# A decode kernel with two attention layers and two small mixers: earlier layer-norm statistics, mixers in halves, 50 idle matmuls and rearranged small constants

## The chip, the cores and the metric

The kernel runs on one core of a Trainium2 chip. Time is device time in microseconds (us). In the views, PE is TensorE, which runs the matmuls, PEld its weight loads (a matmul and its weight load are called a pair below), DVE VectorE, ACT ScalarE, SP the engine that issues the loads, and DMA the 16 engines that carry them out. A "span" is the length of the one profiled execution of a kernel; it is some 1.8 us shorter than the time reported for that execution (539.3 against 541.08 us before). A ratio is the mean time of a kernel's fast runs over that of the kernel before in the same rounds on the same chip, so it is not quite the ratio of the medians quoted beside it. A profile or a chain shows one execution, which need not be the typical one.

## The reference

One token (`x` of 640 values) passes through attention, mixer, attention, mixer, each with a layer norm. Attention uses the last 4096 positions of a cache of 32 heads with 192 values each, so each layer reads 32 K slabs and 32 V slabs of 1.5 MB. Both layers have the same cache and weights.

```python
def _A_ref(x, k_cache, v_cache, wq, wo):           # cut
    q = (x @ wq) ...                               # 32 heads of 192
    k = k_cache[:, :, Sk - W:, :]                  # W = 4096
    v = v_cache[:, :, Sk - W:, :]
    p = softmax(einsum("bhqd,bhkd->bhqk", q, k) * Dh ** -0.5)
    return einsum("bhqk,bhkd->bhqd", p, v) ... @ wo
def _B_ref(x, w1, w2, w3, w4):                     # with S = 1 the shifted parts are zero: x1 = x
    h2 = _gelu(_layernorm(x1) @ w3) @ w4
    return x1 + h2
x = x + _A_ref(_layernorm(x), ...); x = x + _B_ref(_layernorm(x), ...)   # twice
```

## The kernel before

Everything that comes from memory lands in eleven "cells" of 12,288 bytes per partition, handed out again when their reader is done; the query weights and part of the mixer weights have places of their own. Seven transposed K slabs are kept from layer 0 for layer 1. In SBUF the small constants lie ahead of the cells.

```python
const = ctx.enter_context(tc.tile_pool(name="const", bufs=1))
cells = ctx.enter_context(tc.tile_pool(name="cells", bufs=1))      # after const, in SBUF too
wq_sb = const.tile([P, ND, HD], BF16, name="wq_sb")
...
even = const.tile([P, 1], F32, name="even")      # 4 bytes take 32 here: see a_minus32
lo = const.tile([P, 1], F32, name="lo")
maskq = const.tile([P, 4], F32, name="maskq")
blkm = const.tile([P, NM], F32, name="blkm")
...
def give(key):                                   # a cell is free again: the next load may start
    free.append(cell_of.pop(key))
...
def mixer(layer, x_cur, rs_cur, x_new, rs_new):
    xc, xcf, total = ln_center(x_cur, rs_cur)    # mean by a fp32 matmul with ones, then x - mean
    for fc in range(NF):                         # NF = 12, ND = 5: 60 matmuls with w3
        for kc in range(ND):
            nc.tensor.matmul(hT_ps[:, fc:fc + 1], lhsT=w3[kc][...], rhs=xc[:, kc:kc + 1], ...)
        if fc == NF // 3:
            var_ps = total()                     # fp32 matmul: the variance
            rr = power(var_ps, 1.0 + eps, eps2, "rr")
    ...                                          # GELU by exp and reciprocals, on ScalarE and VectorE
    for n in range(ND):                          # 60 matmuls with w4
        for fc in range(NF):
            nc.tensor.matmul(y2_ps[:, n:n + 1], lhsT=w4[fc][...], rhs=hT[:, fc:fc + 1], ...)
```

## Time and profile before

| reading | before |
|---|---|
| time, median of the first 4 runs | 541.01 us (540.15 to 541.38) |
| span of the profiled execution | 539.3 us |
| transfer rate away from start, hand-over and end | 422 GB/s |
| hand-over from layer 0 to layer 1, slices 20 to 24 of 40 | 401, 404, 396, 331, 382 GB/s |
| start of the last output projection, when its last weights had landed, to the end | 10.4 us |

First the page of the kernel before: its span, the rows for busy DMA engines and moved GB/s (40 equal slices of the span), the data queue and the instruction queue (packets, MB, share of 16 engines' span), and the chain of waits by engine.

```profile
span 539.3 us, 14866 instructions
DMA  8999999999999999999999999999999999999992
GB/s 347 427 425 422 419 424 423 423 424 418 422 424 424 418 424 422 421 423 424 401 404 396 331 382 424 419 424 420 427 420 421 422 420 423 420 422 425 422 408 93
q1 hardware_dynamic: 23636, 218.54, 97.7%
q8 instruction: 53, 0.87, 0.7%
DMA 71%; PE 15%; DVE 11%; issue 2%; ACT 1%; SPq 0%; DVEq 0%; ACTq 0%
```

The DMA engines are full nearly everywhere (the data queue's packets fill 97.7% of their span).

In the hand-over the chain of waits of the kernel before (start, length, what) reads as follows. L482 is layer 0's last output projection, L703 mixer 0's second matmuls; "issue" is time in which PE waited for nothing that the profile shows.

```profile
288.43 0.98 PE y_ps L482 x30
...
294.34 1.75 PE y_ps L703 x60
296.29 0.28 issue
...
301.30 1.71 issue
...
306.94 1.45 issue
```

The timeline of the SP engine has the load of the next output-projection weights, which cannot start before layer 1's fourth head gives its cell back:

```profile
308.66 0.33 SPq L143 DMA_DIRECT2D cell<-in_A_wo_dram  x1
```

And the end of the chain: the last output-projection weights land at 528.82 us, then the last output projection (L482), the variance matmul (L288), the first GELU step (L680), the w4 matmuls (L703) and the final fp32 transpose (L721).

```profile
512.83 15.99 DMA cell<-in_A_wo_dram
528.87 0.58 PE y_ps L482 x15
...
531.34 0.43 PE var_ps L288 x2
...
532.79 0.28 ACT sq L680
...
534.35 1.75 PE y_ps L703 x60
...
536.43 0.39 PE row_ps L721
```

### The profile page before, as it was taken

To read this page: it belongs to the slowest core of one execution; us is meant where nothing else is said; L and a number is where in the kernel's file an instruction comes from. 1 tells how busy PE (TensorE), PEld (TensorE's weight loads), DVE (VectorE), ACT (ScalarE), POOL (GpSimd) and SP (SyncE) were. 2 spreads that over 40 slices of the span, in tenths; PEclk is the share of its full clock that TensorE was granted. 3 is DMA by queue.
4 is the path that set the end of the run, shared out by engine and by line. 5 is a ranking of instruction groups with operands and counts; after the bars stand their busy time and mean duration, and the time that the engine had idled before them with its cause. 6 is when DMAs were issued, how large, how long until landed. Compare 5 with 4: busy or idle time off the path is not lost.

```text
span 539.3 us, 14866 instructions
## 1 busy us (share of the span) xinstructions
PE 281.6 (52%) x6820; PEld 229.1 (42%) x6820; DVE 257.4 (48%) x494; ACT 54.6 (10%) x249; POOL 2.0 (0%) x11
## 2 busy tenths in 40 slices
PE   0146556364363644645635777665454654636555
PEld 0045445254353533534424765554343543525434
DVE  2187536455455545546303147665363654545511
ACT  1001010010100101010201011010010101001011
POOL 1000000000000000000000000000000000000000
DMA  8999999999999999999999999999999999999992
GB/s 347 427 425 422 419 424 423 423 424 418 422 424 424 418 424 422 421 423 424 401 404 396 331 382 424 419 424 420 427 420 421 422 420 423 420 422 425 422 408 93
DMA packets 23698, 219.48 MB, mean 407 GB/s; under 512 B 2517, under 2 KB 2901, under 8 KB 8149
## 3 DMA queue, kind: packets, MB, share of 16 engines
q1 hardware_dynamic: 23636, 218.54, 97.7%
q8 instruction: 53, 0.87, 0.7%
q14 instruction: 9, 0.07, 0.0%
HBM read 218.53 MB, written 0.00 MB: 405 GB/s over the span
## 4 chain that ended last, share of the span: by engine, by line
DMA 71%; PE 15%; DVE 11%; issue 2%; ACT 1%; SPq 0%; DVEq 0%; ACTq 0%
DMA cell<-in_A_k_cache_dram 49%; DMA cell<-in_A_v_cache_dram 15%; DVE cell L322 10%; PE O_ps L459 4%; PE ST_ps L372 3%; DMA cell<-in_A_wo_dram 3%; DMA wq_sb<-in_A_wq_dram 3%; PE qT_ps L339 1%; PE y_ps L482 1%; PE nb_ps L402 1%; PE hT_ps L671 1%; PE y_ps L703 1%; PE l_ps L422 1%; DVE o_sb L463 0%; PE PT_ps L417 0%
## 5 line engine op out<-in xcount | busy, mean ns | idle before, releaser
L322 DVE STREAM_TRANSPOSE cell<-cell 128x768 uint32<-128x768 uint32 x228 | 204.6, 946 | 91.5 <-DMA cell<-in_A_k_cache_dram 91.5
L372 PE MATMUL ST_ps<-Qblk,cell 128*128 128x4 bf16 x3072 | 113.4, 168 | 159.3 <-DVE cell L322 155.2
L372 PEld LDWEIGHTS <-cell 128*128 128x128 bf16 x3072 | 97.3, 105 | 189.8 <-DVE cell L322 181.0
L459 PE MATMUL O_ps<-cell,PT 128*1 128x192 bf16 x2048 | 98.3, 359 | 16.7 <-DMA cell<-in_A_v_cache_dram 16.2
L463 DVE STREAM_TRANSPOSE o_sb<-O_ps 128x192 f32<-128x192 f32 x64 | 24.5, 382 | 114.2 <-PE O_ps L459 114.2
L459 PEld LDWEIGHTS <-PT 128*1 128x1 bf16 x2048 | 68.6, 115 | 23.5 <-issue 12.3
L472 ACT ACTIVATE oT<-oT_ps,rl 32x6 bf16<-32x6 f32 x64 | 16.5, 257 | 284.8 <-PE oT_ps L471 284.8
L408 ACT ACTIVATE Pr<-ST_ps,nb_sb,sc 128x32 bf16<-128x32 f32 x64 | 25.1, 488 | 0.5
L471 PE MATMUL oT_ps<-o_sb,Lq 128*32 128x6 f32 x128 | 17.0, 204 | 11.8 <-DVE o_sb L463 11.7
L339 PE MATMUL qT_ps<-xc,wq_sb 128*128 128x1 bf16 x480 | 15.9, 166 | 13.4 <-DMA wq_sb<-in_A_wq_dram 12.9
L339 PEld LDWEIGHTS <-wq_sb 128*128 128x128 bf16 x480 | 15.0, 105 | 14.1 <-DMA wq_sb<-in_A_wq_dram 13.6
L471 PEld LDWEIGHTS oT_ps<-o_sb,Lq 128*32 128x32 f32 x128 | 12.0, 142 | 20.9 <-issue 15.6
L417 PEld LDWEIGHTS <-Eq 128*32 128x32 bf16 x256 | 4.0, 105 | 30.8 <-DVE y_acc L522 25.2
L482 PE MATMUL y_ps<-oT,cell 128*128 128x1 bf16 x480 | 15.3, 166 | 2.9 <-DMA cell<-in_A_wo_dram 1.9
L353 PE MATMUL Qrep_ps<-Xq,Lb 128*128 128x24 bf16 (+1 forms) x18 | 3.2, 180 | 25.3 <-DVE Xq L346 25.0
L482 PEld LDWEIGHTS <-cell 128*128 128x128 bf16 x480 | 14.6, 105 | 3.5 <-DMA cell<-in_A_wo_dram 2.6
L408 ACT ACTIVATION_READ_ACCUMULATOR Pr<-ST_ps,nb_sb,sc 128x1 f32 x64 | 14.4, 224 | 0.0
L404 ACT COPY nb_sb<-nb_ps 128x4 f32<-128x4 f32 x16 | 2.6, 162 | 112.0 <-PE nb_ps L402 112.0
L422 PE MATMUL l_ps<-lpart,ones 128*128 128x4 f32 x32 | 9.4, 365 | 5.3 <-ACT PT L420 5.3
L346 DVE TENSOR_TENSOR Xq<-qT_ps,maskq 128x24 bf16<-128x24 f32 (+1 forms) x18 | 2.8, 155 | 19.5 <-PE qT_ps L339 19.4
L422 PEld LDWEIGHTS l_ps<-lpart,ones 128*128 128x128 f32 x32 | 8.0, 311 | 6.9 <-ACT PT L420 6.7
L402 PE MATMUL nb_ps<-dg,ones 4*128 4x4 f32 x32 | 9.0, 348 | 1.0
(85 smaller groups left out, 107.0 us busy)
## 6 DMA issues: line engine op xcount, KB each, us to landing
cell<-in_A_v_cache_dram SPq DMA_DIRECT2D x59, 1536.0 KB, 28.0
cell<-in_A_k_cache_dram SPq DMA_DIRECT2D x57, 1536.0 KB, 28.1
cell<-in_A_wo_dram SPq DMA_DIRECT2D x14, 960.0 KB, 24.4
wq_sb<-in_A_wq_dram SPq DMA_DIRECT2D x5, 1536.0 KB, 11.0
cell<-in_A_v_cache_dram SPq DMA_DIRECT2D x9, 768.0 KB, 14.4
cell<-in_B_w_dram SPq DMA_DIRECT2D x2, 1280.0 KB, 14.5
cell<-in_A_wo_dram SPq DMA_DIRECT2D x4, 480.0 KB, 15.2
cell<-in_B_w_dram SPq DMA_DIRECT2D x1, 1536.0 KB
```

The costliest lines, as they stand in the source:

```text
L322: nc.vector.transpose(Tu, Ku[:, :, q * NY:(q + 1) * NY])
L339: nc.tensor.matmul(qT_ps[:, tl:tl + 1], lhsT=wq_sb[:, kc, t * P:(t + 1) * P], rhs=xc[:, kc:kc + 1], start=(kc == 0), stop=(kc == ND - 1))
L372: nc.tensor.matmul(ST_ps[:, hq, q * ng + g, :], lhsT=T4[:, g, f, :, t], rhs=Qblk[:, h * NCOL + 2 * f + t, :], start=(n == 0), stop=(n == N ...
L402: nc.tensor.matmul(nb_ps[:], lhsT=ones[0:n, :], rhs=held["dg"][0:n, :], start=True, stop=True)
L408: nc.scalar.activation(out=Pr[:, hq].rearrange("p m g -> p g m"), in_=ST_ps[:, hq], func=ACTF.Exp, bias=nb_sb[:, hq:hq + 1], scale=sc[:, 0 ...
L422: nc.tensor.matmul(l_ps[:], lhsT=ones[:], rhs=held["l"][:], start=True, stop=True)
L459: nc.tensor.matmul(O_ps[r:r + 1, :], lhsT=PT[:, hq, i:i + 1], rhs=V[:, i * Dh:(i + 1) * Dh], start=(i < 4), stop=(i >= NB - 4))
L463: nc.vector.transpose(o_sb[:], O_ps[:].rearrange("p (a c) -> p c a", c=NA))
L471: nc.tensor.matmul(oT_ps[r, :], lhsT=Lq[:], rhs=o_sb[:, :, 0], start=True, stop=True)
L472: nc.scalar.activation(oT[r, :], oT_ps[r, :], ACTF.Copy, scale=rl[r, 0:1])
L482: nc.tensor.matmul(y_ps[:, n:n + 1], lhsT=wo_t[:, k * D + n * P:k * D + (n + 1) * P], rhs=oT[:, k:k + 1], start=(i == 0 if split else k == 0),
L671: nc.tensor.matmul(hT_ps[:, fc:fc + 1], lhsT=w3[kc][:, f0:f0 + 2 * P - 1:2], rhs=xc[:, kc:kc + 1], start=(kc == 0), stop=(kc == ND - 1))
```

## The change

The intent is to shorten both mixers. The last output-projection sum is centred beforehand, so row sum and sum of squares come from a small remainder `z` and both fp32 matmuls stand ahead of the w3 matmuls. The w3 matmuls go in two halves to two PSUM tiles, so that the first half's GELU can overlap PE. The final transpose is bf16 instead of fp32. Fifty idle matmuls, whose results nothing reads, stand at the start. Some small constants share a tile, which makes room for new ones.

```diff
+NORM = (True, True)
+HALF = (True, True)
+BF16_OUT = True
+PAD = 50
 ...
-    even = const.tile([P, 1], F32, name="even")
-    lo = const.tile([P, 1], F32, name="lo")
-    maskq = const.tile([P, 4], F32, name="maskq")
-    blkm = const.tile([P, NM], F32, name="blkm")
+    el = const.tile([P, 2], F32, name="el")
+    even, lo = el[:, 0:1], el[:, 1:2]
+    mb = const.tile([P, 4 + NM], F32, name="mb")
+    maskq, blkm = mb[:, 0:4], mb[:, 4:4 + NM]
 ...
+    def idle_matmuls(n):
+        if n:
+            pad_ps = psm.tile([P, 1], F32, tag="psm")
+            for _ in range(n):
+                nc.tensor.matmul(pad_ps[:], lhsT=Lb[:], rhs=Lb[:, 0:1], start=True, stop=True)
+    idle_matmuls(PAD)
 ...                                       # in add_y: n is the number of sums still to come
+            if n == 1:                    # y so far, with its row sum; later centred to y[1]
+                nc.vector.scalar_tensor_tensor(out=y_new[:], in0=y_ps[:], ..., accum_out=rs[:, 0:1])
+            if n == 0:
+                nc.vector.scalar_tensor_tensor(out=z_new[:], in0=y_ps[:], ..., in1=y[1][:], accum_out=rs_new[:, 0:1])
+                nc.scalar.activation(junk[:], z_new[:], ACTF.Square, accum_out=ss_new[:, 0:1])
 ...                                       # in mixer
+        nc.tensor.matmul(s1_ps[:], lhsT=ones[:], rhs=rs_cur[:, 0:1], start=True, stop=True)
+        nc.tensor.matmul(s2_ps[:], lhsT=ones[:], rhs=ss_cur[:, 0:1], start=True, stop=True)
 ...
+        for half in range(parts):         # two PSUM tiles, then GELU half by half
+            for i in range(HF): ...       # w3
+        order = [(n, half * HF + i) for half in range(parts) for n in range(ND) for i in range(HF)]
 ...
-    x1, x2, x3, x4 = (const.tile([P, ND], F32, name=f"x{i}") for i in range(1, 5))
-    rs1, rs2, rs3 = (const.tile([P, 1], F32, name=f"rs{i}") for i in range(1, 4))
+    x1, x2, x3 = (const.tile([P, ND], F32, name=f"x{i}") for i in range(1, 4))
+    x4 = const.tile([P, ND], out.dtype if BF16_OUT else F32, name="x4")
+    z = [const.tile([P, ND], F32, name=f"z{i}") ...]
+    zs = [const.tile([P, 1], F32, name=f"zs{i}") for i in range(4)]
```

More of the change, by code (lines that the diff above doesn't have):

```diff
@@ L30 @@
 NJ4, NGK, NM = 4, 8, 4
+NORM = (True, True)
+HALF = (True, True)
+BF16_OUT = True
+PAD = 50
+PAD1 = 0
+HOLD = False
 @with_exitstack
@@ L257 @@
     nc.vector.memset(eps1[:], eps)
-    eps2 = const.tile([P, 1], F32, name="eps2")
-    nc.vector.memset(eps2[:], eps * eps)
+    if not all(NORM):
+        eps2 = const.tile([P, 1], F32, name="eps2")
+        nc.vector.memset(eps2[:], eps * eps)
+    for i in range(PAD1):
+        nc.vector.memset(const.tile([P, 1], F32, name=f"gap{i}")[:], 0.0)
     Qblk = const.tile([P, H * NCOL, NM], BF16, name="Qblk")
@@ L269, with shared @@
                             op1=ALU.add, accum_out=rs0[:, 0:1])
+    def shared(name, tag):
+        return dict(name=name, tag=tag) if any(NORM) and not all(HALF) else dict(name=name)
+    def idle_matmuls(n):
[4 more added lines that the diff above has]
+    idle_matmuls(PAD)
     def ln_center(x, rowsum):
@@ L291, in ln_center, with power @@
         return xc, xcf, total
-    def power(var_ps, mul, bias, tag):
+    def power(var, mul, bias, tag):
         ln_t = sm.tile([P, 1], F32, tag=tag + "_ln")
-        nc.scalar.activation(ln_t[:], var_ps[:, 0:1], ACTF.Ln, bias=bias[:], scale=mul / D)
+        nc.scalar.activation(ln_t[:], var, ACTF.Ln, bias=bias, scale=mul)
         r = sm.tile([P, 1], F32, tag=tag)
@@ L487, in out_proj, with attention @@
         return y_ps
-    def attention(layer, x_cur, rs_cur, x_new, rs_new):
+    def attention(layer, x_cur, rs_cur, x_new, z_new, rs_new, ss_new):
         groups = GROUPS[layer]
@@ L492, in attention @@
         y = [x_cur]
+        junk = sm.tile([P, ND], F32, tag="ln_junk")
         Th = {}
@@ L498, in softmax_scale @@
         def softmax_scale():
-            rstd = power(total(), 1.0, eps1, "rstd")
+            rstd = power(total()[:, 0:1], 1.0 / D, eps1[:], "rstd")
             nc.vector.tensor_scalar(out=sc[:], in0=rstd[:], scalar1=scale, scalar2=None, op0=ALU.mult)
@@ L514, in S, with add_y, center @@
                 area[0] = None
-        def add_y(y_ps, last):
-            if last:
-                nc.vector.scalar_tensor_tensor(out=x_new[:], in0=y_ps[:], scalar=1.0, in1=y[0][:],
-                                               op0=ALU.mult, op1=ALU.add, accum_out=rs_new[:, 0:1])
-                return
-            y_new = sm.tile([P, ND], F32, name="y_acc")
-            nc.vector.tensor_add(y_new[:], y[0][:], y_ps[:])
+        def add_y(y_ps, n):
+            if not NORM[layer]:
+                if n == 0:
+                    nc.vector.scalar_tensor_tensor(out=x_new[:], in0=y_ps[:], scalar=1.0, in1=y[0][:],
+                                                   op0=ALU.mult, op1=ALU.add, accum_out=rs_new[:, 0:1])
+                    return
+                y_new = sm.tile([P, ND], F32, name="y_acc")
+                nc.vector.tensor_add(y_new[:], y[0][:], y_ps[:])
+                y[0] = y_new
+                return
+            y_new = x_new if n == 0 else sm.tile([P, ND], F32, name="y_acc")
+            if n == 1:
+                rs = sm.tile([P, 1], F32, **shared("rs_y", "ln_ssq"))
+                nc.vector.scalar_tensor_tensor(out=y_new[:], in0=y_ps[:], scalar=1.0, in1=y[0][:],
+                                               op0=ALU.mult, op1=ALU.add, accum_out=rs[:, 0:1])
+                def center():
+                    nm_ps = psm.tile([P, 1], F32, tag="psm")
+                    nc.tensor.matmul(nm_ps[:], lhsT=ones[:], rhs=rs[:, 0:1], start=True, stop=True)
+                    ym = sm.tile([P, ND], F32, **shared("y_m", "xcf"))
+                    nc.vector.scalar_tensor_tensor(out=ym[:], in0=nm_ps[:, 0:1].broadcast_to([P, ND]),
+                                                   scalar=-1.0 / D, in1=y_new[:], op0=ALU.mult, op1=ALU.add)
+                    y.append(ym)
+                y.append(center)
+            else:
+                if n == 0:
+                    nc.vector.scalar_tensor_tensor(out=z_new[:], in0=y_ps[:], scalar=1.0, in1=y[1][:],
+                                                   op0=ALU.mult, op1=ALU.add, accum_out=rs_new[:, 0:1])
+                    nc.scalar.activation(junk[:], z_new[:], ACTF.Square, accum_out=ss_new[:, 0:1])
+                nc.vector.tensor_add(y_new[:], y[0][:], y_ps[:])
@@ L523, in add_y, with center_y @@
             y[0] = y_new
+        def center_y():
+            if NORM[layer]:
+                y.pop()()
         qa, qb = (qproj_steps(groups[0][0] // QH, xc, part) for part in (0, 1))
@@ L602, in attention @@
                     if pending is not None:
-                        add_y(y_ps, False)
+                        add_y(y_ps, 2)
                         pending = None
@@ L612, in attention @@
                 if layer == 0:
-                    add_y(out_proj(layer, *pending), False)
+                    add_y(out_proj(layer, *pending), 1)
                 PT, rl = early
@@ L621, in attention @@
                 if final:
+                    if layer == 0 and hq == 1:
+                        center_y()
                     fold = None
@@ L655, in attention @@
                 if layer == 1:
-                    add_y(out_proj(layer, *pending), False)
-                fold()
+                    y_ps = out_proj(layer, *pending)
+                    if not NORM[1]:
+                        add_y(y_ps, 1)
+                    fold()
+                    if NORM[1]:
+                        add_y(y_ps, 1)
+                    center_y()
+                else:
+                    fold()
             pending = (cur[0] // QH, oT)
             ST = ST_n
-        add_y(out_proj(layer, *pending), True)
@@ L662, in mixer @@
-    def mixer(layer, x_cur, rs_cur, x_new, rs_new):
+        add_y(out_proj(layer, *pending), 0)
+    def mixer(layer, x_cur, z, rs_cur, ss_cur, x_new, rs_new):
         w3 = need("w3", 0)
-        xc, xcf, total = ln_center(x_cur, rs_cur)
-        hT_ps = psm.tile([P, NF], F32, tag="psm")
-        for fc in range(NF):
-            f0 = 2 * P * (fc // 2) + fc % 2
-            for kc in range(ND):
-                nc.tensor.matmul(
-                    hT_ps[:, fc:fc + 1], lhsT=w3[kc][:, f0:f0 + 2 * P - 1:2], rhs=xc[:, kc:kc + 1],
-                    start=(kc == 0), stop=(kc == ND - 1))
-            if fc == NF // 3:
-                var_ps = total()
-                rr = power(var_ps, 1.0 + eps, eps2, "rr")
-        rg = sm.tile([P, 1], F32, name="rg")
-        nc.vector.tensor_scalar(out=rg[:], in0=rr[:], scalar1=GELU_A * GELU_C, scalar2=None, op0=ALU.mult)
-        sq = sm.tile([P, NF], F32, name="sq")
-        nc.scalar.activation(sq[:], hT_ps[:], ACTF.Square, scale=rr[:, 0:1])
-        gu = sm.tile([P, NF], F32, name="gu")
-        nc.vector.scalar_tensor_tensor(out=gu[:], in0=sq[:], scalar=1.0 / GELU_C, in1=hT_ps[:],
-                                       op0=ALU.add, op1=ALU.mult)
-        ge = sm.tile([P, NF], F32, name="ge")
-        nc.scalar.activation(ge[:], gu[:], ACTF.Exp, scale=rg[:, 0:1])
-        rh = sm.tile([P, NF], F32, name="rh")
-        nc.vector.tensor_scalar(out=rh[:], in0=hT_ps[:], scalar1=rr[:, 0:1], scalar2=None, op0=ALU.mult)
-        nc.vector.reciprocal(rh[:], rh[:])
-        hT = sm.tile([P, NF], BF16, name="hT")
-        nc.vector.scalar_tensor_tensor(out=gu[:], in0=ge[:], scalar=1.0, in1=rh[:],
-                                       op0=ALU.add, op1=ALU.mult)
-        rstd = power(var_ps, 1.0, eps1, "rstd")
-        with nc.allow_low_precision(reason="the matmul's operand, bf16 as in the reference"):
-            nc.vector.reciprocal(hT[:], gu[:])
@@ new lines, in mixer @@
+        stats = []
+        if NORM[layer]:
+            s1_ps = psm.tile([P, 1], F32, tag="psm")
+            nc.tensor.matmul(s1_ps[:], lhsT=ones[:], rhs=rs_cur[:, 0:1], start=True, stop=True)
+            s2_ps = psm.tile([P, 1], F32, tag="psm")
+            nc.tensor.matmul(s2_ps[:], lhsT=ones[:], rhs=ss_cur[:, 0:1], start=True, stop=True)
+            xc = sm.tile([P, ND], BF16, name="xc")
+            xcf = sm.tile([P, ND], F32, name="xcf")
+            for t in (xc, xcf):
+                nc.vector.scalar_tensor_tensor(out=t[:], in0=s1_ps[:, 0:1].broadcast_to([P, ND]), scalar=-1.0 / D,
+                                               in1=z[:], op0=ALU.mult, op1=ALU.add)
+            st = sm.tile([P, 4], F32, **shared("st", "nb_sb"))
+            m2, s2d, b1, b2 = (st[:, i:i + 1] for i in range(4))
+            nc.vector.tensor_scalar(out=b1, in0=s1_ps[:], scalar1=1.0 / D, scalar2=None, op0=ALU.mult)
+            nc.vector.tensor_tensor(out=m2, in0=b1, in1=b1, op=ALU.mult)
+            nc.vector.tensor_scalar(out=b2, in0=m2, scalar1=-(1.0 + eps), scalar2=eps * eps, op0=ALU.mult, op1=ALU.add)
+            nc.vector.scalar_tensor_tensor(out=s2d, in0=s2_ps[:], scalar=1.0 / D, in1=m2, op0=ALU.mult, op1=ALU.max)
+            rr = power(s2d, 1.0 + eps, b2, "rr")
+            rg = sm.tile([P, 1], F32, **shared("rg", "sc"))
+            nc.vector.tensor_scalar(out=rg[:], in0=rr[:], scalar1=GELU_A * GELU_C, scalar2=None, op0=ALU.mult)
+            nc.vector.tensor_scalar(out=b1, in0=m2, scalar1=-1.0, scalar2=eps, op0=ALU.mult, op1=ALU.add)
+        else:
+            xc, xcf, total = ln_center(x_cur, rs_cur)
@@ new lines, in mixer @@
+        parts = 2 if HALF[layer] else 1
+        HF = NF // parts
+        hT = sm.tile([P, NF], BF16, name="hT")
+        h_ps = []
+        for half in range(parts):
+            if HALF[layer]:
+                hp = psS.tile([P, 4, NGK, NM], F32, name="ST_ps")
+                hp = hp[:, 0].rearrange("p g m -> p (g m)")[:, 0:HF]
+            else:
+                hp = psm.tile([P, NF], F32, tag="psm")
+            for i in range(HF):
+                fc = half * HF + i
+                f0 = 2 * P * (fc // 2) + fc % 2
+                for kc in range(ND):
+                    nc.tensor.matmul(
+                        hp[:, i:i + 1], lhsT=w3[kc][:, f0:f0 + 2 * P - 1:2], rhs=xc[:, kc:kc + 1],
+                        start=(kc == 0), stop=(kc == ND - 1))
+                if fc == NF // 3 and not NORM[layer]:
+                    var_ps = total()
+                    rr = power(var_ps[:, 0:1], (1.0 + eps) / D, eps2[:], "rr")
+            h_ps.append(hp)
@@ new lines, in mixer @@
+        if not NORM[layer]:
+            rg = sm.tile([P, 1], F32, **shared("rg", "sc"))
+            nc.vector.tensor_scalar(out=rg[:], in0=rr[:], scalar1=GELU_A * GELU_C, scalar2=None, op0=ALU.mult)
+        for half, hp in enumerate(h_ps):
+            WF = NF // 2 if all(HALF) else NF
+            sq, gu, ge, rh = (sm.tile([P, WF], F32, name=n)[:, 0:HF] for n in ("sq", "gu", "ge", "rh"))
+            nc.scalar.activation(sq, hp[:] if not HALF[layer] else hp, ACTF.Square, scale=rr[:, 0:1])
+            hpa = hp[:] if not HALF[layer] else hp
+            nc.vector.scalar_tensor_tensor(out=gu, in0=sq, scalar=1.0 / GELU_C, in1=hpa,
+                                           op0=ALU.add, op1=ALU.mult)
+            nc.scalar.activation(ge, gu, ACTF.Exp, scale=rg[:, 0:1])
+            nc.vector.tensor_scalar(out=rh, in0=hpa, scalar1=rr[:, 0:1], scalar2=None, op0=ALU.mult)
+            nc.vector.reciprocal(rh, rh)
+            nc.vector.scalar_tensor_tensor(out=gu, in0=ge, scalar=1.0, in1=rh,
+                                           op0=ALU.add, op1=ALU.mult)
+            with nc.allow_low_precision(reason="the matmul's operand, bf16 as in the reference"):
+                nc.vector.reciprocal(hT[:, half * HF:(half + 1) * HF], gu)
@@ L696, in mixer @@
+        if NORM[layer]:
+            rstd = power(s2d, 1.0, b1, "rstd")
+        else:
+            rstd = power(var_ps[:, 0:1], 1.0 / D, eps1[:], "rstd")
         base = sm.tile([P, ND], F32, name="base")
@@ L700, in mixer @@
         y2_ps = psm.tile([P, ND], F32, tag="psm")
-        for n in range(ND):
-            for fc in range(NF):
-                nc.tensor.matmul(
-                    y2_ps[:, n:n + 1], lhsT=w4[fc][:, n * P:(n + 1) * P], rhs=hT[:, fc:fc + 1],
-                    start=(fc == 0), stop=(fc == NF - 1))
+        order = [(n, half * HF + i) for half in range(parts) for n in range(ND) for i in range(HF)]
+        for i, (n, fc) in enumerate(order):
+            nc.tensor.matmul(
+                y2_ps[:, n:n + 1], lhsT=w4[fc][:, n * P:(n + 1) * P], rhs=hT[:, fc:fc + 1],
+                start=(i == 0 if HALF[layer] else fc == 0),
+                stop=(i == len(order) - 1 if HALF[layer] else fc == NF - 1))
         give(("w4", layer))
@@ L711, in mixer @@
                                            op0=ALU.mult, op1=ALU.add, accum_out=rs_new[:, 0:1])
-    x1, x2, x3, x4 = (const.tile([P, ND], F32, name=f"x{i}") for i in range(1, 5))
-    rs1, rs2, rs3 = (const.tile([P, 1], F32, name=f"rs{i}") for i in range(1, 4))
-    attention(0, xT, rs0, x1, rs1)
-    mixer(0, x1, rs1, x2, rs2)
-    attention(1, x2, rs2, x3, rs3)
-    mixer(1, x3, rs3, x4, None)
-    row_ps = psm.tile([ND, P], F32, tag="psm")
-    nc.tensor.transpose(row_ps[:, :], x4[:, :], ident[:, :])
+    x1, x2, x3 = (const.tile([P, ND], F32, name=f"x{i}") for i in range(1, 4))
+    x4 = const.tile([P, ND], out.dtype if BF16_OUT else F32, name="x4")
+    rs2 = const.tile([P, 1], F32, name="rs2")
+    z = [const.tile([P, ND], F32, name=f"z{i}") if NORM[i] else None for i in range(2)]
+    zs = [const.tile([P, 1], F32, name=f"zs{i}") for i in range(4)]
+    attention(0, xT, rs0, x1, z[0], zs[0], zs[1])
+    mixer(0, x1, z[0], zs[0], zs[1], x2, rs2)
+    attention(1, x2, rs2, x3, z[1], zs[2], zs[3])
+    mixer(1, x3, z[1], zs[2], zs[3], x4, None)
+    row_ps = psm.tile([ND, P], out.dtype if BF16_OUT else F32, tag="psm")
+    nc.tensor.transpose(row_ps[:, :], x4[:, :], Eq[:].rearrange("p j b -> p (j b)") if BF16_OUT else ident[:, :])
     o_fin = const.tile([ND, P], out.dtype, name="o_fin")
```

## The prediction

> **What bounds it now.** The span is 539.3 us. The queue part of the page has the data queue's packets at 97.7% of the 16 DMA engines' span; slices hold 420 to 425 GB/s except in two places. Slices 20 to 23 (the hand-over from layer 0 to layer 1) fall to 401, 404, 396, 331, 382; two-microsecond windows show 271 to 380 GB/s from 296 to 316 us, about 4.4 us of lost transfer. And the end: after the last output-projection weights land at 528.8 us, only compute is left, 10.5 us in the chain of waits. The change alters no bytes, so its gain can only come from those two places.
>
> **The tail, layer 1 (timeline).** Before: z/x at 529.47, mean matmul, xc, 60 w3 matmuls from 530.53 to 532.69 with the fp32 variance matmul costing 0.43 us in their midst, GELU chain 532.79 to 534.34 with PE idle 1.65 us, 60 w4 matmuls 1.75 us, x4 at 536.13, fp32 transpose 0.37 us, copy, DMA out. After: row sum and sum of squares come from a pre-centred z, so both fp32 matmuls go before the w3 matmuls, while PE waits for xc anyway (0.43 us gained; PE starts w3 at about the same time). Centring y takes one fp32 matmul (about 0.58 us) while the last projection weights are awaited, hence nothing. rr is known near 531.6, so the first half's GELU starts at about 531.65, 1.1 us earlier. The second half's chain follows on ACT and DVE and ends near 534.2; the first 30 w4 matmuls are hidden under it, leaving 30 (0.87 us) instead of 60. x4 near 535.1: 1.0 us gained. The bf16 transpose gives another 0.15 to 0.2. The w4 transfer ends at 532, so it doesn't hold the earlier start. Tail: about 1.15 us.
>
> **The hand-over.** Mixer 0 is on the chain too (288.4 to 296.3), and K/V transfers of layer 1 starve behind it, so its 1.0 us should reach the DMA. But here the chain has "issue" stalls of PE: 0.28 us before the mean matmul, 1.71 us at 301.3, 1.45 us at 306.9. Exactly 128 load/matmul pairs lie between them, so I read them as instruction fetch[...]. The 50 idle pairs at the start cost nothing (PE waits there for wq until 10.98 and 22.05 us), but move those boundaries 52 pairs earlier against the work: into w4, then the 17th and 65th pair-stretches of layer 1's first scores. My estimate is stalls of the same kind, total 2.5 to 4 us against 3.4. So the hand-over gains 0 to 2 us, probably 0.9.
>
> **Prediction.** 541.0 - 1.15 - 0.9, about 538.9 us; range 537.7 to 540.3. Faster by over 2%: 0.01; within 2%: 0.98; slower by over 2%: 0.01.
>
> **What would show it.** Chain of waits: from the last projection weights' landing to the end 9.3 to 9.4 us instead of 10.5; in the timeline first w4 matmul near 4.4 us after that landing (was 5.5), a second idle of PE before the second 30; transpose about 0.2 us. Windows of 2 us from the hand-over: less lost transfer; the last DMA landing about 0.9 us earlier. PE idle for "issue" at new positions, still 128 pairs apart. DMA bytes equal.
>
> **What would make it wrong.** Refill stalls falling into mixer 0 or adding up to more; a stall in the tail; the second half's GELU running serially behind the first longer than estimated; starvation in the hand-over that is set by the transposes rather than the mixer.

541.0 - 1.15 (tail) - 0.9 (hand-over) comes to 538.95 us. The trace of the kernel before shows a queue of the kind "instruction" (q8) with 53 packets of 16,384 bytes, one for each 257 of the 13,640 weight loads and matmuls that the page counts, and, by the matmul records, 128 pairs between the ends of the waits at 303.01 and 308.38 us. The 0.15 to 0.2 us for the transpose is an estimate: there the fp32 transpose took 0.37 us (L721), a bf16 transposing matmul of the attention 0.19 us (L417).

## More of the kernel before

Next, the windows view of the kernel before in two steady stretches; columns are the window, its length, busy time and instructions of PE, PEld, DVE, ACT and POOL, the granted clock, DMA share and GB/s.

```profile
30.00:240.00 210.00, 108.96 (x2656) 88.96 (x2656) 115.27 (x194) 18.63 (x86) 0.00 (x0) 1.00 1.01 422
340.00:500.00 160.00, 84.55 (x2054) 68.70 (x2047) 85.98 (x147) 15.13 (x70) 0.00 (x0) 1.00 1.01 422
```

## The result

The changed kernel takes 530.67 us (median of 8 runs, 530.57 to 531.08) against 541.25 us (13 runs); the ratio is 0.9806, interval 0.9797 to 0.9816. That is 10.6 us less, where 2.1 was predicted, and outside the range of 537.7 to 540.3.

The same parts of the page of the changed kernel:

```profile
span 529.1 us, 15002 instructions
DMA  8999999999999999999999999999999999999993
GB/s 349 429 428 426 424 431 427 429 429 426 428 424 430 426 428 429 427 430 426 412 405 413 384 405 428 424 429 424 429 427 427 430 425 431 426 427 429 425 420 134
q1 hardware_dynamic: 23636, 218.54, 98.1%
q8 instruction: 54, 0.88, 0.6%
DMA 70%; PE 13%; DVE 13%; issue 2%; ACT 1%; SPq 0%; DVEq 0%
```

The rate is higher in nearly every slice, not only around the mixers. The windows view of the changed kernel in the same stretches:

```profile
30.00:240.00 210.00, 111.30 (x2700) 90.94 (x2701) 115.92 (x195) 19.73 (x92) 0.00 (x0) 1.00 1.01 427
340.00:500.00 160.00, 88.77 (x2144) 71.99 (x2142) 90.22 (x153) 15.43 (x72) 0.00 (x0) 1.00 1.01 428
```

That is 427 and 428 GB/s instead of 422, with DMA share 1.01 in both: the engines were not busier, each packet took less time (between 30 and 240 us, a packet of 12,288 bytes took 467 ns on average before and 462 after). The hand-over in the chain of waits of the changed kernel (L502 is the last output projection, L800 the w4 matmuls):

```profile
284.54 0.95 PE y_ps L502 x30
...
289.08 1.85 PE y_ps L800 x60
...
298.36 1.61 issue
...
303.74 1.89 issue
...
310.67 1.61 issue
```

And SP's timeline there, with the V load and the output-projection load that answers to the one shown of before:

```profile
300.33 0.33 SPq L136 DMA_DIRECT2D cell<-in_A_v_cache_dram  x1
301.63 0.33 SPq L149 DMA_DIRECT2D cell<-in_A_wo_dram  x1
```

It starts 17.1 us after layer 0's last output projection (301.63 - 284.54), against 20.2 (308.66 - 288.43). The end of the chain:

```profile
504.15 15.57 DMA cell<-in_A_wo_dram
519.77 0.57 PE y_ps L502 x15
...
520.59 0.60 PE s_ps L729 x2
...
522.56 0.28 ACT sq L777
...
524.30 1.85 PE y_ps L800 x60
...
526.38 0.28 PE row_ps L822
```

From the last output projection to the end of the span, before took 539.3 - 528.87 = 10.4 us, the changed kernel 529.1 - 519.77 = 9.3 us. The first GELU step (L777) comes 2.8 us after that projection instead of 3.9, and the bf16 transpose takes 0.28 us as a chain piece instead of 0.39.

Adding up the packet records gives the time at which a given number of MB had been moved, and so where the 10.2 us between the two spans lie:

| stretch | before, us | changed, us | less |
|---|---|---|---|
| 0 to 120 MB (layer 0) | 289.3 | 285.8 | 3.5 |
| 120 to 135 MB (hand-over) | 40.1 | 37.4 | 2.7 |
| 135 to 215 MB (layer 1) | 190.6 | 188.2 | 2.4 |
| 215 MB to the end | 19.3 | 17.7 | 1.6 |

The 5.9 us in the first and third rows lie where no line of the mixers runs.

### The profile page after: what moved, and what is told of

It reads as the page before. It is cut to its first block, busy times and chain, and to the rows that moved or that the text cites. A ratio compares the mean times of both kernels' runs of the same rounds, so it can differ in the third digit from the quotient of the medians.

```text
span 529.1 us, 15002 instructions
## 1 busy us (share of the span) xinstructions
PE 284.2 (54%) x6874; PEld 231.3 (44%) x6874; DVE 260.1 (49%) x519; ACT 55.7 (11%) x253; POOL 2.0 (0%) x11
## 3 DMA queue, kind: packets, MB, share of 16 engines
q1 hardware_dynamic: 23636, 218.54, 98.1%
## 4 chain that ended last, share of the span: by engine, by line
DMA 70%; PE 13%; DVE 13%; issue 2%; ACT 1%; SPq 0%; DVEq 0%
DMA cell<-in_A_k_cache_dram 54%; DVE cell L342 11%; DMA cell<-in_A_v_cache_dram 10%; PE O_ps L479 4%; PE ST_ps L392 3%; DMA cell<-in_A_wo_dram 3%; DMA wq_sb<-in_A_wq_dram 3%; PE qT_ps L359 1%; PE y_ps L502 1%; PE nb_ps L422 1%; PE y_ps L800 1%; PE l_ps L442 1%; DVE o_sb L483 0%; DVE cell L468 0%; PE oT_ps L491 0%
## 5 line engine op out<-in xcount | busy, mean ns | idle before, releaser
L492 ACT ACTIVATE oT<-oT_ps,rl 32x6 bf16<-32x6 f32 x64 | 16.4, 257 | 281.4 <-PE oT_ps L491 281.4
L491 PE MATMUL oT_ps<-o_sb,Lq 128*32 128x6 f32 x128 | 16.9, 204 | 11.4 <-DVE o_sb L483 11.2
L491 PEld LDWEIGHTS oT_ps<-o_sb,Lq 128*32 128x32 f32 x128 | 12.0, 141 | 20.1 <-issue 15.6
L502 PE MATMUL y_ps<-oT,cell 128*128 128x1 bf16 x480 | 15.2, 166 | 2.3 <-DMA cell<-in_A_wo_dram 1.5
L502 PEld LDWEIGHTS <-cell 128*128 128x128 bf16 x480 | 14.7, 105 | 2.9 <-DMA cell<-in_A_wo_dram 2.1
L366 DVE TENSOR_TENSOR Xq<-qT_ps,mb 128x24 bf16<-128x24 f32 (+1 forms) x18 | 2.8, 154 | 20.4 <-PE qT_ps L359 20.3
```

Of the source, the lines that this page charges most:

```text
L491: nc.tensor.matmul(oT_ps[r, :], lhsT=Lq[:], rhs=o_sb[:, :, 0], start=True, stop=True)
L492: nc.scalar.activation(oT[r, :], oT_ps[r, :], ACTF.Copy, scale=rl[r, 0:1])
L502: nc.tensor.matmul(y_ps[:, n:n + 1], lhsT=wo_t[:, k * D + n * P:k * D + (n + 1) * P], rhs=oT[:, k:k + 1], start=(i == 0 if split else k == 0),
```

## The experiments

Two theories stood at the start. A: the rate rose because the cells now start at another byte. B: the mixers and the idle matmuls shift the schedule, and that raised the rate.

### The kernel before with the cells 32 bytes further (b_plus32)

```diff
-    o_fin = const.tile([ND, P], out.dtype, name="o_fin")
+    o_fin = const.tile([ND, P + 16], out.dtype, name="o_fin")[:, 0:P]
```

The last constant is 32 bytes longer, no instruction changes.

> The kernel before with one edit: the last constant tile is 32 bytes longer per partition, so every K/V/weight buffer (cell) starts at a multiple of 512 bytes in its partition instead of 480 past one, as in the changed kernel; no instruction changes. Theory A (placement: the 1.3% higher transfer rate outside the hand-over comes from where the cells start): slices at 427 to 430 GB/s instead of 420 to 425 and a time of 532 to 535 us. Theory B (the mixer and the idle matmuls, by shifting the schedule, raise the rate): no change, 540.5 to 541.9 us.

Measured: 534.31 us (4 runs), ratio 0.9862 (0.9841 to 0.9883). The windows of this kernel:

```profile
30.00:240.00 210.00, 111.06 (x2700) 90.91 (x2701) 116.32 (x196) 19.61 (x92) 0.00 (x0) 1.00 1.01 427
340.00:500.00 160.00, 86.25 (x2100) 70.31 (x2100) 89.63 (x150) 15.41 (x71) 0.00 (x0) 1.00 1.01 427
```

One tile, made longer, carries 7.5 us (1.38% of 541.25) and the rise of the rate. Theory A is shown; B falls as the cause of the higher rate.

### The changed kernel with the cells where they were (a_minus32)

```diff
-    el = const.tile([P, 2], F32, name="el")
+    el = const.tile([P, 3], F32, name="el")
-    eps1 = const.tile([P, 1], F32, name="eps1")
+    eps1 = el[:, 2:3]
```

> The changed kernel with the constant eps1 put into another small tile, so that the cells start again 480 bytes past a multiple of 512, everything else as changed. Theory A: slices fall back to 420 to 425 GB/s, time 538 to 540 us, about what the prediction had. Theory B: stays at 530 to 531.5 us.

Measured: 537.64 us (5 runs), ratio 0.9925 (0.991 to 0.994); just below the expected 538 to 540. The windows:

```profile
30.00:240.00 210.00, 109.02 (x2651) 88.80 (x2652) 115.15 (x194) 18.65 (x86) 0.00 (x0) 1.00 1.01 422
340.00:500.00 160.00, 86.37 (x2095) 70.24 (x2084) 88.17 (x149) 15.27 (x71) 0.00 (x0) 1.00 1.01 422
```

The rate is back at 422. In the changed kernel, placement is worth 1.19% (0.9925 - 0.9806), 6.4 us. With the cells left in place, the rest of the change gains 0.75%, 4.1 us; between the two kernels with aligned cells it is 0.56% (0.9862 - 0.9806), 3.0 us.

### How aligned (b_plus64, a_plus64, probe)

b_plus64 makes `o_fin` 64 bytes longer in the kernel before, so cells start 32 past a multiple of 512; a_plus64 does that in the changed kernel, where they then start 64 past one. The probe only loads: the same slabs into cells starting at a multiple of 512 plus an offset, 13 loads per offset. Its output is wrong, which doesn't matter for the time. Three forms of theory A were set against each other: A1, the cost grows with the distance above the multiple of 256 below; A2, a multiple of 64 is enough; A3, every start off a multiple of 256 costs the same.

```diff
+OFFS = [0, 480, 224, 192, 128, 96, 64, 32, 256, 0]
+    for off in OFFS:
+        for i in range(13):
+            t = cells.tile([P, FREE + 256], BF16, ...)
+            nc.sync.dma_start(t[:, off // 2:off // 2 + FREE], src[...])
```

> The kernel before with 64 bytes more: cells start 32 bytes past a multiple of 512. Theory A1[...]: most of the gain stays, 533 to 536 us. Theory A2 (any start that is not a multiple of 64 bytes costs the same): as before, 540 to 542 us. Theory B: as before too.

> Transfers only, no compute, wrong output on purpose: 130 loads of the same K and V slabs in ten phases of 13 loads, by the start of the destination within its partition: 0, 480, 224, 192, 128, 96, 64, 32, 256, 0 bytes past a multiple of 512. Theory A1[...]: 0 and 256 fastest, 480 and 224 slowest[...], the others in proportion to the distance from 256 below. Theory A2 (64-byte): 0, 64, 128, 192, 256 equal and fast, 32, 96, 224, 480 slow alike. Theory A3[...]: all but 0 and 256 slow alike. Theory B: all phases alike within 0.3%.

> The changed kernel with the last constant tile 64 bytes longer, so cells start 64 bytes past a multiple of 512. Theory A3 (the transfers need a multiple of 256; the probe had 426.4 GB/s at 64 against 430.0 at 0): 537 to 538.5 us and slices near 422 GB/s, like a_minus32. Theory A2 (a multiple of 64 bytes is enough): 530.3 to 531.3 us.

Measured: b_plus64 541.82 us, ratio 0.9992 (0.9968 to 1.0016): no gain at 32. a_plus64 536.23 us, ratio 0.9911 (0.9894 to 0.9927): most of the gain is gone at 64, and its median is a little below the 537 expected. Its windows:

```profile
30.00:240.00 210.00, 109.34 (x2662) 89.00 (x2660) 115.49 (x195) 18.62 (x86) 0.00 (x0) 1.00 1.01 423
340.00:500.00 160.00, 87.28 (x2115) 70.97 (x2113) 88.91 (x150) 15.39 (x71) 0.00 (x0) 1.00 1.01 423
```

Lines of the windows view of the probe (here only DVE and POOL are listed before clock, share and GB/s); the offsets are 0, 480, 128, 64, 32 and 256 in this order:

```profile
5.00:46.00 41.00, 0.00 (x0) 0.00 (x0) 1.00 1.01 429
53.00:94.00 41.00, 0.00 (x0) 0.00 (x0) 1.00 1.01 426
...
197.00:238.00 41.00, 0.00 (x0) 0.00 (x0) 1.00 1.01 426
...
293.00:334.00 41.00, 0.00 (x0) 0.00 (x0) 1.00 1.01 426
341.00:382.00 41.00, 0.00 (x0) 0.00 (x0) 1.00 1.01 425
389.00:430.00 41.00, 0.00 (x0) 0.00 (x0) 1.00 1.01 429
```

By the starts of ten loads within each phase, the rates are 430.0 GB/s at 0 and 256, 425.9 at 480, 425.2 at 224, 426.2 at 192, 426.4 at 128, 426.1 at 96, 426.4 at 64 and 425.2 at 32. The median packet of 12,288 bytes took 460 ns at 0 and 256 and 462 to 465 ns elsewhere (in the full kernels 464 before and 460 in the changed one). So the step is at multiples of 256 bytes. It is nearly flat, 0.8 to 1.1%, and not in proportion to the distance from the multiple below. Theories A1 and A2 fall, A3 stands in the main, and no engine other than the DMA is needed for it. The small differences recur: 64 past costs less than 32 or 224 past in the probe, and a_plus64 lost less than a_minus32 in the full kernel.

A cost that follows the distance is not seen: the probe has 425.2 both at 32 and at 224 past a multiple of 256. What inside a transfer costs the time was not shown. In the full kernels the step was about 1.3% (427 or 428 against 422; 423 with the cells 64 past). Why it is a little larger there than in the probe (1.1% at 224, the same distance above a multiple of 256 as the cells of the kernel before), where no engine reads SBUF, stays open.

### The 50 idle matmuls (a_nopad, a_pad_only)

a_nopad is the changed kernel without them. a_pad_only is the opposite: old mixers, sums and transpose, the 50 kept. In both, cells stay at a multiple of 512, in a_pad_only by a longer `o_fin`.

```diff
-PAD = 50            # a_nopad
+PAD = 0
-NORM = (True, True) # a_pad_only, and BF16_OUT = False
-HALF = (True, True)
+NORM = (False, False)
+HALF = (False, False)
```

> The changed kernel without the 50 idle matmuls at the start, cells still at a multiple of 512. Theory F (the idle matmuls earn their place by moving the points where PE waits for its next block of instructions in the hand-over): 531.3 to 532.7 us. Theory M (the hand-over's gain comes from the new mixer alone): 530.2 to 531.2 us.

> Changed kernel with its switches set so that both mixers, the additions and the final transpose are the old ones, the 50 idle matmuls kept, cells at a multiple of 512: the aligned kernel of before plus idle matmuls. Theory F: 532.4 to 533.6 us, better than the aligned kernel of before (534.3). Theory M: 534.0 to 534.7 us.

Measured: a_nopad 532.73 us, ratio 0.9843 (0.9825 to 0.9861), its four runs spread from 531.16 to 533.07, the median 0.03 us above the band of F; without the idle matmuls the changed kernel loses 1.4 us (against the ratio of a_again, below) to 2.0 us (against 0.9806). a_pad_only 532.51 us, ratio 0.9845 (0.983 to 0.9859), against 0.9862 for the aligned kernel of before: 0.9 us, with overlapping intervals. Theory F is supported, M falls. The chain of a_nopad, of its slowest run, shows what the idle matmuls move away:

```profile
288.62 1.78 PE y_ps L800 x58
290.40 1.90 issue
292.30 0.23 PE y_ps L800 x2
...
297.51 0.72 issue
...
302.17 2.25 issue
```

A wait of 1.90 us stands after the 58th of the 60 w4 matmuls, inside mixer 0. In the changed kernel these 60 run without one (289.08, 1.85 us), and the first wait comes in layer 1's scores. The waits are 128 load/matmul pairs, 256 instructions, apart, as the prediction read them: by the matmul records 128 lie between the ends of the waits at 303.01 and 308.38 us before, 128 and 127 between those at 299.97, 305.62 and 312.29 us in the changed kernel. Packet records of a queue of their own (q8, kind "instruction") show blocks of 16,384 bytes, 53 before and 54 in the changed kernel; in the kernel before one was moved from 300.64 for 0.97 us and PE went on at 303.01. That these blocks are what PE waited for is read from these times, not tested apart. The longest single wait is 2.73 us, in the chain of a_pad_only. A chain of 50 matmuls that computes nothing earns 1 to 2 us, most likely by where it puts these boundaries.

### The old mixer in layer 0 alone (a_l0old), halving off (a_nohalf), and the changed kernel again

```diff
-NORM = (True, True)      # a_l0old
-HALF = (True, True)
+NORM = (False, True)
+HALF = (False, True)
-HALF = (True, True)      # a_nohalf
+HALF = (False, False)
```

> Changed kernel with the old additions and mixer in layer 0 alone, new ones in layer 1, cells at a multiple of 512. The tail keeps its 1.1 us. If the rest of the 3.6 us between the aligned kernel of before and the changed one comes from mixer 0 and what follows it: 532.6 to 533.4 us. If it comes from elsewhere (the start, the idle matmuls): 530.6 to 531.4 us.

> The changed kernel with its halving of the mixers switched off in both layers (early statistics stay), cells at a multiple of 512. If halving is worth what the prediction's tail sum had (the second 30 of 60 w4 matmuls instead of all, 0.87 us, and the GELU starting before the last w3 matmuls, 0.8 us, less the longer serial chain, about 0.6): 0.6 to 1.1 us slower per mixer where PE's block waits don't interfere, 531.9 to 532.9 us in all. If the early statistics carry the tail: under 0.5 us slower.

> The changed kernel itself, unedited, on the same chip as the three below, so that they can be compared within one set of rounds: 530.2 to 531.2 us.

Measured: a_l0old 531.57 us, ratio 0.9829 (0.9814 to 0.9844), between the two expected bands and nearer to the lower. Against the changed kernel's 0.9806, mixer 0 is worth 1.2 us with the waits as they fell, against a_again's 0.9817 0.7 us; against a_pad_only's 0.9845, in the same rounds, the new layer 1 with its bf16 transpose is worth 0.9 us. a_nohalf 531.58 us, ratio 0.9828 (0.9813 to 0.9843), against a_again 530.84 us, 0.9817 (0.9803 to 0.983), in the same rounds: 0.7 us by the medians for both mixers together, between the two expectations. The intervals of the ratios overlap, but the slowest run of a_again (531.38) is below the fastest of a_nohalf (531.42). In the profiles, halving took about 0.5 us from the tail (9.8 us from the last projection to the end without it, 9.3 with it) and 0.8 us from PE's path in the hand-over (table below); not all of it became time.

### Other numbers of idle matmuls (a_pad125, a_pad40, a_pad120)

> The changed kernel with 125 idle matmuls instead of 50: the 256-instruction boundaries move 75 load/matmul pairs earlier, one of them out of the middle of layer 1's first scores to the wait for xc before its first projection. By theory F and the waits of the changed kernel's trace (a block ready some 5.7 us after the one before was entered), the hand-over gains 0 to 0.4 us: 530.2 to 530.8 us, and PE's waits for issue move 75 pairs earlier, none in a w3 or w4 matmul. If the boundaries don't matter: 530.4 to 530.9, with waits at random places.

(The 5.7 us is the distance between the ends of the first two waits of the changed kernel's hand-over, 299.97 and 305.62 us.)

Measured: 532.49 us, ratio 0.9845 (0.9832 to 0.9859), 1.7 us slower than a_again in the same rounds. The expectation was missed. The chain's waits in the hand-over were only these two, 3.05 us in sum, less than the 5.1 us of the changed kernel (1.61, 1.89, 1.61):

```profile
296.26 0.80 issue
...
301.00 2.25 issue
```

The second one stands 3 pairs before the end of the fourth head, which frees the cell for the next output-projection load. That suggested theory G: a wait counts by the load it holds back. Two more numbers put it to the test.

> The changed kernel with 120 idle matmuls. With 125, one boundary lay 3 pairs before the end of the fourth head, which frees the cell for the next output-projection load. Five pairs later it lies 2 pairs behind that end. Theory G: that load starts about 2.2 us earlier than with 125 (17 us instead of 18.7 after the start of layer 0's last output projection), the next K load as with 125; 530.8 to 531.9 us against 532.5. Theory F1: as with 125, 532.2 to 532.8 us.

> The changed kernel with 40 idle matmuls. In the changed kernel PE's first wait for a block lies 6 load/matmul pairs before the end of layer 1's third head, whose end lets the next V load start, so that load waits too. Ten pairs later for every boundary puts the wait just behind that end. Theory G (a block wait costs only as far as it delays a load while the queue is running dry): that V load starts 1.6 to 2.2 us earlier relative to the last output projection of layer 0, later loads as before, 529.5 to 530.4 us. Theory F1 (all waits of the hand-over count by their sum): the sum does not change, 530.5 to 531.1 us.

Measured: a_pad120 532.82 us, ratio 0.9839 (0.9815 to 0.9863). Its four runs are 530.73, 532.41, 533.23 and 533.64. The profiled one is the fastest, and in it that load did start 17.1 us after the projection, as G has it; the others have no profile, and the median missed G's band. a_pad40 530.86 us, ratio 0.9808 (0.9792 to 0.9824): the V load started earlier as intended (14.6 us after the last projection of layer 0, instead of 15.8 and 16.4 in the two profiles with 50), but the load after it 0.6 to 1.2 us later, and the time did not move. So G's simple form is not confirmed. Its rival F1 (all waits of the hand-over count by their sum) had the medians within its band in a_pad40 and 0.02 us above it in a_pad120, but a_pad125, slower with a smaller sum of waits, speaks against it. One regularity does hold: with 0, 120 and 125 idle matmuls, which are within 8 pairs of the same place in a period of 128, the medians are 532.73, 532.82 and 532.49 us, with 40 and 50 they are 530.86 and 530.67. That fits boundaries 128 pairs apart, and not an effect that grows with the number of idle matmuls. What the profiles also show is this sum, from the start of layer 0's last output projection to the start of that output-projection load:

| kernel | us to that load | "issue" waits of PE before it | remainder |
|---|---|---|---|
| before | 20.2 | 3.4 | 16.8 |
| b_plus32 | 21.3 | 4.5 | 16.8 |
| a_pad_only | 18.4 | 1.5 | 16.9 |
| a_l0old | 19.2 | 2.3 | 16.9 |
| a_nopad | 20.7 | 4.9 | 15.8 |
| changed | 17.1 | 1.6 | 15.5 |
| a_again | 17.7 | 2.3 | 15.5 |
| a_nohalf | 18.0 | 1.7 | 16.3 |
| a_pad125 | 18.7 | 3.1 | 15.6 |
| a_pad120, profiled run | 17.1 | 1.5 | 15.6 |

The remainder is PE's path itself: 16.8 with the old mixer 0, 15.5 with the new, 1.3 us less, and 16.3 with halving off. The waits vary from 1.5 to 4.9 us with where the boundaries fall. Each row is one execution: that of a_pad120 is the fastest of four, that of a_nopad the slowest. How much of a wait becomes time is not settled beyond that.

### The other weights aligned too (a_wq256, a_best)

The query weights and the rest of the mixer weights start 128 past a multiple of 256. A gap of 128 bytes moves them; five small constants share a tile to pay for it.

```diff
+    gap = const.tile([P, 32], F32, name="gap")
+    nc.vector.memset(gap[:, 0:1], 0.0)
     wq_sb = const.tile([P, ND, HD], BF16, name="wq_sb")
 ...
-    rs2 = const.tile([P, 1], F32, name="rs2")
+    zall = const.tile([P, 5], F32, name="zall")
+    rs2 = zall[:, 4:5]
-    zs = [const.tile([P, 1], F32, name=f"zs{i}") for i in range(4)]
+    zs = [zall[:, i:i + 1] for i in range(4)]
```

> The changed kernel with the query weights and the rest of the mixer weights moved by 128 bytes to a multiple of 256 as well (five small constants share one tile to pay for it, cells stay at a multiple of 512). Theory A3: the first 7.9 MB run about 1% faster, 0.15 to 0.25 us in all, 530.3 to 530.6 us; within the noise at best. If placement mattered only for the cells: no change.

> 40 idle matmuls and the query weights at a multiple of 256 together: under theory G 529.2 to 530.1 us, faster than the changed kernel; under F1 530.3 to 530.8 us.

Measured: a_wq256 530.48 us, ratio 0.9805 (0.9791 to 0.982), 0.4 us below a_again in the same rounds by the medians, with overlapping intervals: unclear. a_best, which is this with 40 idle matmuls, 530.62 us, ratio 0.9804 (0.9787 to 0.9821): level with a_pad40 in its rounds, short of G's band. (Its profiled execution had a granted clock of 0.81 and yet a span of 528.7 us.) No version clearly beats the changed kernel.

## Why the prediction was wrong

- **"The change alters no bytes, so its gain can only come from those two places."** This step failed: it took the transfer rate elsewhere as fixed. Bytes were equal (218.54 MB on the data queue in both), but the rate was not a constant of the kernel. Placement is a third term, sized zero in the prediction, and measured 6.4 to 7.5 us of 10.6 us (a_minus32 against the changed kernel, and b_plus32).
- **Tail, "about 1.15 us".** Right: 10.4 to 9.3 us in the chain, and 0.9 us by a_l0old against a_pad_only. The first GELU step came 2.8 us after the last projection began (predicted about 2.8), the first w4 matmul after 4.5 (predicted 4.4). The second idle of PE that was predicted before the second 30 w4 matmuls had all but vanished: the 60 took 1.85 us instead of 1.75.
- **Mixer 0, "its 1.0 us should reach the DMA".** About right: PE's path lost 1.3 us, and a_l0old puts 0.7 to 1.2 us in time on it.
- **"The 50 idle pairs at the start cost nothing".** True at the start (PE waits for the query weights in both kernels, four times, up to 3.5 us), but the benefit from moving the waits was mis-sized: it was put at none (2.5 to 4 us of waits against 3.4), and measured 1.4 to 2.0 us in the changed kernel, 0.9 us with the old mixers (with overlapping intervals). The prediction read the spacing of 128 pairs rightly, and then estimated only the sum of the waits. The chain has 5.1 us in the changed kernel, more than estimated; but only 1.6 us of them stand ahead of the output-projection load, against 3.4 us before. That the start of such loads is what counts was our reading (theory G), and a_pad40 and a_pad120 did not confirm it.
- **Hand-over, "0 to 2 us, probably 0.9".** Without placement, tail and hand-over together were 3.0 to 4.1 us, so the hand-over gained some 2 to 3 us, at or above the end of its range. With placement undone (a_minus32), the change measured 537.64 us where the prediction said 538.9: its own mechanisms account for some 1.3 us of the 8.2 us by which it missed (1.7 us if the ratio 0.9925 is taken in place of the median).

## What to carry to other kernels

When a transfer-bound kernel's diff touches any allocation, list the start of every transfer's destination in both built programs before costing anything: here a start off a multiple of 256 bytes cost 1.3% of the rate (422 against 427 or 428 GB/s), and one longer tile won most of the gain. Where PE runs without gaps and loads wait for its results, as in the hand-over here, look for waits 128 load/matmul pairs apart as in these traces: inserting or removing instructions far away moved them, and the time by 1 to 2 us. A change that bundles several small edits is best judged after undoing each one alone.
